# Attention and a silu feed-forward layer on one core: h of batches 2 to 7 by block products, and attention moved into the out layer's time

## The chip, the cores and the metric

The kernel runs on one core of a Trainium2 chip. Five engines work side by side, each through its own queue in order: PE (matrix products, with a weight-load queue PEld), DVE and ACT (element by element; ACT also has the sigmoid and silu tables), POOL (element by element, and it issues the loads) and SP (it issues transposes and stores). The metric is the device time of one execution in microseconds (us), here the median of several; smaller is better. A profiled execution also gives the span from the first to the last instruction.

## The reference

Eight batches of attention with 12 heads, 448 positions and 64 columns a head; the weights are a sigmoid, not a softmax. Then a feed-forward layer on 3584 rows:

```python
scores = scale * np.matmul(q, k.transpose(0, 1, 3, 2)) - np.log(S)   # S = 448
attn = 1.0 / (1.0 + np.exp(-scores))
x = np.matmul(attn, v).transpose(0, 2, 1, 3).reshape(B * S, H * D)   # 3584 x 768
h = x @ w_in                                                         # 768 x 2048
g = h * (1.0 / (1.0 + np.exp(-h)))
out = g @ w_out                                                      # 2048 x 768
```

## The kernel before

**Attention.** A quad is four heads of one batch; there are 24, numbered through the batches, three to a batch. Its q, k and v are loaded by POOL (`load`, line 71), as f16. The first quads' q and k are transposed on PE (`pe_transpose`), from quad 6 on by DMA: `dma_transpose` (line 158) copies rows together on ACT or DVE and SP issues the transpose. A unit is one of seven chunks of a quad's 448 keys: `scores(g, ch)` (line 169) makes four 64x64 matmuls into a score buffer `psc` (two buffers) and ACT takes the sigmoid into `attnT` (12 buffers). `values(g)` (line 193) multiplies seven chunks with v into two banks `pav`, and DVE copies them scaled into `xT` (line 218), the transposed x of a batch: six chunks of 128 columns by 448 positions. Buffers `pav`, `ph` and `po` share four PSUM banks (pool `ps_1`).

**h.** `h_unit(b, fc)` (line 229) makes one of 16 column groups of h of a batch: six matmuls over the chunks of x into `ph`; ACT takes the sigmoid, DVE multiplies it with `ph` into `gTr` (line 248), which holds g of two neighbouring batches.

**The out layer.** `out_set` (line 288) makes two row blocks of 128 rows of out at once by seven block products of eight matmuls each instead of eight (a Strassen scheme in Winograd's form): the operands are the quarters of `w_out` and of two blocks of g, with sums of them in `T1` to `T4` (`w_sums`, made once by DVE) and in `S1` to `S4` (made by DVE for each set). ACT copies the first product as `m1`; DVE adds the others up (`plus`, line 313) in `osb`, and SP stores `osb`. A pair of batches has seven row blocks, so three sets and one block left over; the left-over of an even pair is kept in `kept` and taken with that of the next pair: 14 sets.

**The order.** PE's order is written out by hand. `all_moe` (line 379) is one stream of the matmuls of h and the out layer, for a pair m of batches: h(2m), for m > 0 then the first set, h(2m+1), the other sets. `stretch(ns)` (line 398) takes as many matmuls of that stream as make ns (189 a matmul of h, 163 of out). The main loop at line 541 takes two units of scores, then perhaps one quad's values, perhaps one row copy (`rows_if_any`), then a stretch as long as `paces` says; before quad 6 (n = 42) it takes a stretch of 21500. After that, attention runs two batches ahead of h and lies in stretches of 2 to 3.4 us through h and out alike. POOL's order of loads follows from `after_transpose` and `after_values` (lines 431 and 440); POOL has eight loads under way at most.

Of the kernel before, what the change touches and what calls it, by code (L numbers as in the profile page):

```python
# [17 lines left out]
def kernel(  # L18
# [104 lines left out]
    def new_qkT(g):  # L123
        for name in ("k", "q"):
            qkT[name, g] = p4.tile([P, NCH, P], F16, tag=f"{name}T", name=f"{name}T")
# [32 lines left out]
    def dma_transpose(g, name, copy):  # L158
        if ("k", g) not in qkT:
            new_qkT(g)  # L160
        rows = p3.tile([P, NCH, 2, D], F16, tag=f"{name}r", name=f"{name}r")
# [31 lines left out]
    def values(g, end=NCH):  # L193
# [23 lines left out]
        for half in range(2):  # L217
            nc.vector.tensor_scalar_mul(xT[b][:, half * NQ + iq, :], pav[half][:, :S], SX)  # L218
# [10 lines left out]
    def h_unit(b, fc):  # L229
# [16 lines left out]
        tsig = p3.tile([P, S], F16, tag="tsig", name="tsig")  # L246
# [4 lines left out]
        yield 189  # L251

# [35 lines left out]
    def out_set(a1, rows1, a2, rows2, last=False):  # L288
        nonlocal hold
        lo, hi = slice(0, NHC), slice(NHC, NFC)  # L290
        osb = [p4.tile([P, DMODEL], F32, tag="osb", name="osb") for _ in range(2)]
        c11, c12 = (osb[0][:, nh * NO2 : (nh + 1) * NO2] for nh in range(2))
        c21, c22 = (osb[1][:, nh * NO2 : (nh + 1) * NO2] for nh in range(2))
        m1 = p2.tile([P, NO2], F32, tag="m1", name="m1")
        sg = [cpool.tile([P, NHC, P], F16, tag=f"S{i}", name=f"S{i}") for i in range(1, 5)]
# [7 lines left out]
        def product(a, w):  # L303
            po = ps_1.tile([P, 512], F32, tag="ps1", name="po")
            for fc in range(NHC):
# [3 lines left out]
                if fc < NHC - 1:  # L309
                    yield 163  # L310
            return po[:, :NO2]

        def plus(o, po, x, sign=ISX):
            nc.vector.scalar_tensor_tensor(  # L314
                out=o, in0=po, scalar=sign, in1=x, op0=ALU.mult, op1=ALU.add
            )

        nc.vector.tensor_sub(sg[2], a1[:, lo], a2[:, lo])
        nc.vector.tensor_add(sg[0], a2[:, lo], a2[:, hi])
        po = yield from product(a1[:, lo], wq[0][0])  # L320
        nc.scalar.activation(m1, po, AF.Copy, scale=ISX)  # L321
        nc.vector.tensor_sub(sg[1], sg[0], a1[:, lo])
        hold = False
        yield 163
        po = yield from product(a1[:, hi], wq[1][0])
# [5 lines left out]
        po = yield from product(sg[2], tw[3])  # L331
        plus(c22, po, m1)
        yield 163
# [5 lines left out]
        plus(c21, po, c22, -ISX)  # L339
# [15 lines left out]
    by_h1 = {3: 6, 6: 7, 9: 8}  # L355
    early = [h_unit(0, fc) for fc in range(2)]
    sums = w_sums()

    def moe_h(b):
# [71 lines left out]
    def after_transpose(g):  # L431
# [5 lines left out]
        elif g == 4:  # L437
            load("kq", 8)
# [153 lines left out]
```

## Time and profile before

| what | value |
|---|---|
| median of 3 runs | 381.67 us (380.77 to 382.28) |
| the profiled execution | 381.95 us |
| its span | 380.2 us, clock granted 1.00 |
| matmuls | 3083: 768 of h, 784 of out, 672 of scores, 672 of values, 168 transposes, 19 warm-ups |
| bytes moved by DMA | 42.80 MB, mean 113 GB/s |

How to read the profile's lines: a group is "line engine operation out<-in, shapes, xcount | busy us, mean ns of one | idle us of the engine just before them, and who ended it". The chain of work that ended last is "start us, us, engine, tile, line, xcount", in order of time. A wait is "engine, tile <- who was waited for: us in all, times, longest". The timeline is "start, us, engine, line, operation, tiles, shapes, xcount [idle before <- who ended it]". The durations of neighbours on one engine can overlap, as the next one enters while the last one drains.

### The profile page before, as it was taken

What the parts mean: (1) busy time and instruction counts of PE and PEld (TensorE: products, weight loads), DVE (VectorE), ACT (ScalarE), POOL (GpSimd) and SP (SyncE); (2) the same over time, 40 slices, a digit from 0 to 9 for tenths busy, and PEclk for the clock granted to TensorE, in tenths of its full rate; (3) what the DMA queues carried; (4) which work ended last, traced back from release to release, by engine and by line L of the source; (5) the groups of instructions that cost most, each with busy time, mean ns of one, the idle gap of its engine ahead of it and who ended that gap; (6) DMA issues with size and microseconds to landing.
All of it is one profiled execution on the core that took longest, in us unless ns stands there. A gap on an engine that the chain in (4) does not pass through costs nothing.

```text
span 380.2 us, 7666 instructions
## 1 busy us (share of the span) xinstructions
PE 370.8 (98%) x3083; PEld 186.0 (49%) x3083; DVE 235.2 (62%) x416; ACT 225.9 (59%) x329; POOL 93.5 (25%) x158
## 2 busy tenths in 40 slices
PE   7989999999999999999999999999999999999995
PEld 2444445545554445445555444544455444555563
DVE  2636646987565666566766647735757446656773
ACT  4988875757667764777434576477764776054000
POOL 8946325403752323122221303101100000000000
PEclk9999999999999999999999999999999999999999
DMA  7999999995999947945939949536347300110233
GB/s 125 177 185 204 205 204 171 133 140 110 165 241 216 151 56 99 173 54 69 162 67 183 132 78 121 71 86 74 48 85 97 84 3 2 50 34 0 82 85 83
DMA packets 66403, 42.80 MB, mean 113 GB/s; under 512 B 37056, under 2 KB 62912, under 8 KB 66368
## 3 DMA queue, kind: packets, MB, share of 16 engines
q0 software_dynamic: 28032, 22.59, 43.2%
q1 hardware_dynamic: 38112, 19.41, 28.5%
q8 instruction: 24, 0.39, 0.4%
q10 hardware_dynamic: 224, 0.33, 0.3%
q14 instruction: 11, 0.09, 0.1%
HBM read 45.61 MB, written 11.01 MB: 149 GB/s over the span
## 4 chain that ended last, share of the span: by engine, by line
PE 78%; DMA 13%; POOL 3%; DVE 3%; ACT 2%; issue 1%; ACTq 0%; POOLq 0%
PE po L306 34%; PE ph L235 29%; PE psc L176 8%; PE pav L207 6%; DMA w_in_sb<-in_moe_w_in_dram 5%; DMA w_out_sb<-in_moe_w_out_dram 5%; DMA qf<-in_q_dram 1%; DMA vf<-in_v_dram 1%; POOL kf L78 1%; DVE gTr L248 1%; DVE T L277 1%; POOL qf L78 1%; ACT qr L137 1%; POOL vf L78 1%; ACT attnT L183 0%
## 5 line engine op out<-in xcount | busy, mean ns | idle before, releaser
L183 ACT ACTIVATE attnT<-psc 128x896 f16<-128x896 f32 x168 | 144.2, 918 | 59.9 <-PE psc L176 59.8
L235 PE MATMUL ph<-xT,w_in_sb 128*128 128x448 f16 x768 | 153.2, 353 | 1.2 <-DMA w_in_sb<-in_moe_w_in_dram 1.2
L248 DVE TENSOR_TENSOR gTr<-ph,tsig 128x448 f16<-128x448 f32 x128 | 78.9, 623 | 70.1 <-ACT tsig L247 68.6
L235 PEld LDWEIGHTS <-w_in_sb 128*128 128x128 f16 x768 | 71.9, 98 | 77.1 <-issue 12.8
L247 ACT ACTIVATE tsig<-ph 128x448 f16<-128x448 f32 x128 | 68.6, 547 | 54.4 <-PE ph L235 53.7
L78 POOL DMA_DIRECT2D vf<-in_v_dram x48 | 28.9, 624 | 136.4 <-PE pav L207 136.4
L306 PEld LDWEIGHTS <-S 128*128 128x128 f16 x448 | 42.3, 98 | 33.9 <-issue 6.8
L314 DVE SCALAR_TENSOR_TENSOR osb<-po,osb 128x384 f32<-128x384 f32 x70 | 37.6, 554 | 25.2 <-PE po L306 24.5
L176 PE MATMUL psc<-qT,kT 64*64 64x448 f16 x672 | 50.7, 362 | 0.9 <-ACT attnT L183 0.3
L218 DVE TENSOR_SCALAR xT<-pav 128x448 f16<-128x448 f32 x48 | 27.7, 619 | 31.4 <-PE pav L207 31.4
L306 PE MATMUL po<-T,S 128*128 128x384 f16 x224 | 40.6, 327 | 0.1
L306 PEld LDWEIGHTS <-gTr 128*128 128x128 f16 x304 | 28.7, 98 | 23.4 <-issue 5.0
L306 PE MATMUL po<-w_out_sb,S 128*128 128x384 f16 x224 | 39.9, 326 | 0.0
L207 PE MATMUL pav<-attnT,vf 64*64 64x448 f16 x672 | 37.5, 349 | 0.2 <-DVE gTr L248 0.2
L78 POOL DMA_DIRECT2D qf<-in_q_dram x46 | 27.7, 613 | 39.4 <-DVE qr L162 16.7
L306 PE MATMUL po<-w_out_sb,gTr 128*128 128x384 f16 x192 | 34.7, 327 | 0.0
L78 POOL DMA_DIRECT2D kf<-in_k_dram x50 | 30.3, 618 | 7.8 <-DVE kr L162 4.3
L176 PEld LDWEIGHTS <-kT 64*64 64x64 f16 x672 | 14.2, 104 | 31.0 <-issue 29.0
L207 PEld LDWEIGHTS <-vf 64*64 64x64 f16 x672 | 20.1, 107 | 12.3 <-issue 1.5
L314 DVE SCALAR_TENSOR_TENSOR osb<-po,m 128x384 f32<-128x384 f32 x42 | 23.1, 551 | 3.9 <-PE po L306 2.5
L306 PE MATMUL po<-T,gTr 128*128 128x384 f16 x112 | 21.4, 326 | 0.0
L321 ACT ACTIVATE m<-po 128x384 f32<-128x384 f32 x14 | 6.9, 492 | 24.0 <-PE po L306 24.0
(41 smaller groups left out, 130.8 us busy)
## 6 DMA issues: line engine op xcount, KB each, us to landing
out_dram<-osb SPq DMA_DIRECT2D x54, 192.0 KB, 3.0
vf<-in_v_dram POOLq DMA_DIRECT2D x48, 112.0 KB, 4.4
kf<-in_k_dram POOLq DMA_DIRECT2D x46, 112.0 KB, 5.4
qf<-in_q_dram POOLq DMA_DIRECT2D x46, 112.0 KB, 5.8
w_in_sb<-in_moe_w_in_dram POOLq DMA_DIRECT2D x4, 768.0 KB, 10.6
w_out_sb<-in_moe_w_out_dram POOLq DMA_DIRECT2D x4, 768.0 KB, 17.1
kT<-kr SPq DMA_TRANSPOSE x18, 5.8
qT<-qr SPq DMA_TRANSPOSE x18, 5.6
```

The source lines that it names most:

```text
L78: nc.gpsimd.dma_start(flat[name, g][half * HP : (half + 1) * HP, :, c0:c1].rearrange("p i c d -> p i (c d)"), source[name][b, h0 : h0 + 2] ...
L137: nc.scalar.activation(o, i, AF.Copy)
L176: nc.tensor.matmul(psc[own, j, :S], qkT["k", g][rows, ch, own], qkT["q", g][rows, :, own], start=True, stop=True,)
L183: nc.scalar.activation(attnT[g, ch], psc[:, :, :S], AF.Sigmoid, bias=NEG_LOG_S, scale=QKSCALE)
L207: nc.tensor.matmul(pav[half][j * D : (j + 1) * D, :S], flat["v", g][own, j, ch, :], at[own, j, :], start=(ch == 0), stop=(ch == NCH - 1),)
L218: nc.vector.tensor_scalar_mul(xT[b][:, half * NQ + iq, :], pav[half][:, :S], SX)
L235: nc.tensor.matmul(ph[:, :S], w_in_sb[:, cc, fc * P : (fc + 1) * P], xT[b][:, cc, :], start=(at == 0), stop=(at == NCC - 1),)
L247: nc.scalar.activation(tsig, ph[:, :S], AF.Sigmoid, bias=0.0, scale=ISX)
L248: nc.vector.tensor_mul(gTr[:, fc, (b % 2) * S : (b % 2) * S + S], ph[:, :S], tsig)
L306: nc.tensor.matmul(po[:, :NO2], a[:, fc, :], w[:, fc, :], start=(fc == 0), stop=(fc == NHC - 1))
L314: nc.vector.scalar_tensor_tensor(out=o, in0=po, scalar=sign, in1=x, op0=ALU.mult, op1=ALU.add)
L321: nc.scalar.activation(m1, po, AF.Copy, scale=ISX)
```

## The change

- h of the pairs m = 1, 2, 3 is made by `h_pair` for both batches at once, with seven block products over quarters of `w_in` and of x of the two batches. Each of its eight rounds makes a column group of 128 of the upper and of the lower half: seven products of three matmuls, where two batches by two column groups by six chunks were 24. g of a round comes from four silus on ACT and five f32 adds on DVE, and a copy of the first product on ACT. Part of a round (`late`) is taken in the next round, and that of the last round in the first product of the first out set (`between`). h of batches 0 and 1 is made as before.
- Sums of `w_in` (`w_in_sums`): six operations on POOL, between loads, three on DVE in h of batch 0, three on DVE in place after h of batch 1. Sums of x (`x_sums`): four on DVE for each chunk pair of a pair of batches, in buffers of `attnT`.
- No attention is taken inside `h_pair`. The units of the next pair's batches lie in the out sets of the pair before, and values in two pieces of four and three rounds. Before quad 6 there is a stretch of 12500 instead of 21500.
- ACT's table changes to silu ahead of each `h_pair` and back to sigmoid behind it: seven table loads instead of one.
- The out set behind `h_pair` gets its first sums made inside the loop, and takes its second and third products in the other order. `kept` is made on DVE instead of ACT; one of twelve xT copies of a later pair is on ACT.
- Loads: the four pieces of `w_out` in another order, two of them and q and k of quads 6 and 7 each behind one of POOL's sums; q and k of quad 9 after the transposes of quad 5, from quad 10 on when the rows of the quad two before are copied. Row copies of quads 6 to 8 begin in h of batch 0 instead of h of batch 1; later ones start within the quad three before instead of after its values.
- Buffers: transposed q and k three instead of four, rows two instead of three, `osb` three instead of four; `m1`, `tsig` and the new copies share three.

The diff, cut to its core:

```diff
         for half in range(2):
-            nc.vector.tensor_scalar_mul(xT[b][:, half * NQ + iq, :], pav[half][:, :S], SX)
+            if b > 2 and b % 2 == 1 and iq == NQ - 1 and half == 0:
+                nc.scalar.activation(
+                    xT[b][:, half * NQ + iq, :], pav[half][:, :S], AF.Copy, scale=SX
+                )
+            else:
+                nc.vector.tensor_scalar_mul(xT[b][:, half * NQ + iq, :], pav[half][:, :S], SX)
+        if b > 2 and b % 2 == 1:
+            x_sums(b // 2, iq)
...
+    def x_sums(m, iq):
+        b11, b21 = (xT[2 * m][:, half * NQ + iq, :] for half in range(2))
+        b12, b22 = (xT[2 * m + 1][:, half * NQ + iq, :] for half in range(2))
+        t = [p12.tile([P, 2, S], F16, tag="attnT", name="xs") for _ in range(2)]
+        t1, t2, t3, t4 = (t[i // 2][:, i % 2, :] for i in range(4))
+        for o, x, y in ((t1, b12, b11), (t2, b22, t1), (t4, b21, t2), (t3, b22, b12)):
+            nc.vector.tensor_sub(o, x, y)
+        xs[m, iq] = t1, t2, t3, t4
...
+        sw[3] = a21
+        for c in range(HCC):
+            eng = nc.vector if c == HCC - 1 else nc.gpsimd
+            eng.tensor_add(sw[1][:, c], a21[:, c], a22[:, c])
+            yield
+            eng.tensor_sub(sw[2][:, c], sw[1][:, c], a11[:, c])
+            yield
+            eng.tensor_sub(sw[4][:, c], a12[:, c], sw[2][:, c])
+            yield
+        for c in range(HCC):
+            nc.vector.tensor_sub(sw[3][:, c], a11[:, c], a21[:, c])
...
+        sides = {
+            1: (w_in_sb[:, lo, top], lambda c: x[0][:, c, :]),
+            2: (w_in_sb[:, hi, top], lambda c: x[0][:, HCC + c, :]),
+            3: (sw[4], lambda c: x[1][:, HCC + c, :]),
+            4: (w_in_sb[:, hi, low], lambda c: xs[m, c][3]),
+            5: (sw[1], lambda c: xs[m, c][0]),
+            6: (sw[2], lambda c: xs[m, c][1]),
+            7: (sw[3], lambda c: xs[m, c][2]),
+        }
+        def product(n, ps, i, first):
+            a, bs = sides[n]
+            for c in range(HCC):
+                nc.tensor.matmul(
+                    ps,
+                    a[:, c, i * P : (i + 1) * P],
+                    bs(c),
+                    start=(first and c == 0),
+                    stop=(c == HCC - 1),
+                    skip_group_check=True,
+                )
+                yield 189
+        def silu(side, odd, i, src):
+            nc.scalar.activation(
+                gTr[:, side * NHC + i, odd * S : (odd + 1) * S], src, AF.Silu, scale=ISX
+            )
+        def late(i, y, z, p1, u2, u3):
+            silu(1, 1, i, u3)
+            if m < B // 2 - 1 and i < 4:
+                rows_of_quad(
+                    2 * NQ * (m + 1) + 1 + i // 2,
+                    "kq"[i % 2],
+                    (act_copy, nc.vector.tensor_copy)[i % 2],
+                )
+            yield from product(3, z, i, False)
+            nc.vector.tensor_add(u2, z, u2)
+            silu(0, 1, i, u2)
+            yield from product(4, y, i, False)
+            nc.vector.tensor_add(p1, y, p1)
+            silu(1, 0, i, p1)
+        sg = []
+        begun = {}
+        def begin(i):
+            xb = ps_1.tile([P, 512], F32, tag="ps1", name="hx")[:, :S]
+            yield from product(1, xb, i, True)
+            p1 = p3.tile([P, S], F32, tag="m1", name="p1")
+            nc.scalar.activation(p1, xb, AF.Copy)
+            begun[i] = xb, p1
+        EARLY = NHC - 2
+        behind = None
+        yield from begin(0)
+        for i in range(NHC):
+            end = i == NHC - 1
+            if not end:
+                yield from begin(i + 1)
+            xb, p1 = begun[i]
+            y = ps_sc.tile([P, 2, 512], F32, tag="pssc", name="hy")[:, 0, :S]
+            yield from product(6, y, i, True)
+            u2 = p3.tile([P, DMODEL], F32, tag="osb", name="u2")[:, :S]
+            nc.vector.tensor_add(u2, y, p1)
+            if end:
+                nc.vector.tensor_add(behind[5], behind[2], behind[5])
+                set_sums(sg, 2, 0, EARLY)
+            z = ps_1.tile([P, 512], F32, tag="ps1", name="hz")[:, :S]
+            yield from product(5, z, i, True)
+            if behind is not None and not end:
+                yield from late(*behind)
+            yield from product(2, xb, i, False)
+            silu(0, 0, i, xb)
+            yield from product(7, y, i, False)
+            u3 = cpool.tile([P, S], F32, tag="S2" if end else "S4", name="u3")
+            nc.vector.tensor_add(u3, y, p1)
+            if i == EARLY:
+                for s in (1, 3):
+                    sg.append(cpool.tile([P, NHC, P], F16, tag=f"S{s}", name=f"S{s}"))
+            else:
+                nc.vector.tensor_add(u3, z, u3)
+            if end:
+                yield from late(*behind)
+                set_sums(sg, 2, EARLY)
+                set_sums(sg, 0, 0, EARLY)
+            behind = i, y, z, p1, u2, u3
+        sg.insert(1, cpool.tile([P, NHC, P], F16, tag="S2", name="S2"))
...
+        def rest():
+            yield from late(*behind)
+            nc.scalar.activation(warm, warm, AF.Sigmoid)
+            set_sums(sg, 0, EARLY)
+            set_sums(sg, 1)
+            h_done.update((2 * m, 2 * m + 1))
...
+        if tail:
+            po = yield from product(sg[2], tw[3])
+            plus(c22, po, m1)
...
+    rows_at = {14: (6, "k"), 16: (6, "q"), 18: (7, "k"), 21: (7, "q"), 24: (8, "k"), 28: (8, "q")}
...
+            if b == 0 and fc >= NFC - 3:
+                next(in_sums)
             if b == 1:
-                if fc >= 2:
-                    next(sums)
-                if fc in by_h1:
-                    for name in ("k", "q"):
-                        dma_transpose(by_h1[fc], name, act_copy)
-
-    def moe_set(m, g):
-        step = out_set(block(g), row_blocks(m, g), block(g + 1), row_blocks(m, g + 1))
+                next(sums)
+                if fc == 9:
+                    first_sg.extend(
+                        cpool.tile([P, NHC, P], F16, tag=f"S{i}", name=f"S{i}") for i in (1, 2, 3)
+                    )
+                if fc in (9, 11, 13):
+                    set_sums(first_sg, {9: 2, 11: 0, 13: 1}[fc])
+            if b * NFC + fc in rows_at:
+                rows_of_quad(*rows_at[b * NFC + fc], act_copy)
...
+                nc.vector.tensor_scalar_mul(kept[:, fcs], block(NCH - 1)[:, fcs], scale)
+            if m == 0 and g == 2 and i in (36, 44, 52):
+                next(in_sums)
...
+            tail = []
             if m == 0:
-                yield from moe_set(m, 0)
+                yield from moe_h(0)
+                yield from moe_h(1)
+                tail = [None, *first_sg]
+            else:
+                yield from h_pair(m, tail)
+            yield from moe_set(m, 0, tail)
...
+            load_w_out(1, 0)
+            load_w_out(1, 1)
         elif g == 2:
             load("v", 5)
-            load_w_out(1, 0)
-            load_w_out(1, 1)
-            load("kq", 6)
-            load("kq", 7)
+            for what in ("k", 6), ("q", 6), (0, 1), ("k", 7), ("q", 7), (0, 0):
+                next(in_sums)
+                (load_w_out if what[0] == 0 else load)(*what)
...
+    def rows_of_quad(g, name, copy):
+        dma_transpose(g, name, copy)
+        if name == "q" and 7 < g < NQB - 2:
+            load("kq", g + 2)
...
+    PACE, BURST, ROUND, SPARE = 1600, 590, 200, 2400
+    sets = 7 * NHC * 163
+    h_at = [(2 * NFC * NCC - 8) * 189 + 3 * sets]
+    for m in (1, 2):
+        h_at.append(h_at[-1] + 7 * NHC * HCC * 189 + (3 + m % 2) * sets)
+    AHEAD = 4
+    ends = [2 * NT_B, 4 * NT_B + AHEAD, 6 * NT_B + AHEAD, 8 * NT_B]
+    values_left = 2 * NT_B
+    stretch(PACE)
     for n in range(NT_B + 3, len(units), 2):
         burst = units[n : n + 2]
         if n == 2 * NT_B:
             values_if_any()
-            stretch(21500)
+            stretch(12500)
         for u in burst:
             scores(*u)
-        values_if_any()
+        had = values_if_any()
         rows_if_any()
         for g, ch in burst:
+            if ch == NCH - 3 and g >= 6 and g % 6 < 4 and g + 3 < NQB:
+                later.extend(((g + 3, "k"), (g + 3, "q")))
             if ch == NCH - 1:
-                waiting.append(g)
+                waiting.extend(((g, 0, NCH),) if n < 2 * NT_B else ((g, 0, 4), (g, 4, NCH)))
         if n in (24, 30):
             transposes(4 + (n - 24) // 6, "k")
         elif n in (26, 32):
             transposes(4 + (n - 26) // 6, "q")
-        stretch(paces[1] if 1 not in ready else paces[n // NT_B])
-    for g in waiting:
-        values(g)
+        if n < ends[0]:
+            stretch(PACE)
+            continue
+        m = bisect.bisect(ends, n)
+        if n + 2 == ends[m]:
+            nc.scalar.activation(warm, warm, AF.Silu)
+        dense = h_at[m - 1] - SPARE - done
+        due = done
+        stretch((dense + values_left * ROUND) / ((ends[m] - n) // 2) - had * ROUND)
+        values_left -= had
+        if n + 2 == ends[m]:
+            while waiting:
+                values_if_any()
+                stretch(SPARE / 3)
+            values_left = 2 * NT_B
+            while 2 * m not in h_done:
+                done += next(stream)
+            due = done
+            stretch(3000)
```

More of the change, by code (lines that the diff above doesn't have):

```diff
@@ L245, in h_unit @@
             h_done.add(b)
[L246 removed]
+        tsig = p3.tile([P, 2 * S], F16, tag="m1", name="tsig")[:, :S]
         nc.scalar.activation(tsig, ph[:, :S], AF.Sigmoid, bias=0.0, scale=ISX)
@@ L330, in out_set @@
         yield 163
-        po = yield from product(sg[2], tw[3])
-        plus(c22, po, m1)
-        yield 163
+        if not tail:
+            po = yield from product(sg[2], tw[3])
+            plus(c22, po, m1)
+            yield 163
         po = yield from product(sg[1], tw[2])
@@ L391, in all_moe @@
                 yield from out_set(
-                    kept, row_blocks(m - 1, g), block(g), row_blocks(m, g), m == B // 2 - 1
+                    kept,
+                    row_blocks(m - 1, g),
+                    block(g),
+                    row_blocks(m, g),
+                    1.0,
+                    last=(m == B // 2 - 1),
                 )
```

108 lines of the change are left out of this document (64 added, 44 removed).

## The prediction, on record before the result

> **What bounds the kernel now.** I read the page's shares and slices first, then the chain of work that ended last in order of time, then the waits.
>
> ```profile
> span 380.2 us, 7666 instructions
> PE 370.8 (98%) x3083; PEld 186.0 (49%) x3083; DVE 235.2 (62%) x416; ACT 225.9 (59%) x329; POOL 93.5 (25%) x158
> PEclk9999999999999999999999999999999999999999
> PE 78%; DMA 13%; POOL 3%; DVE 3%; ACT 2%; issue 1%; ACTq 0%; POOLq 0%
> ```
>
> PE is busy 98% at the full granted clock; DVE and ACT have some 40% to spare. A busy PE may still be waiting, so the chain has to tell.
>
> ```profile
> 57.30 5.39 DMA qf<-in_q_dram
> 79.29 0.50 PE psc L176 x8
> 115.61 2.56 PE ph L235 x13
> 118.17 0.50 PE psc L176 x8
> 121.93 1.32 PE pav L207 x28
> 330.33 18.16 PE ph L235 x96
> 348.49 27.31 PE po L306 x168
> 375.83 0.56 DVE osb L314
> ```
>
> Loads are in the chain until 63 us; from 79 us to 375.8 it is almost wholly matmuls. 96 h matmuls in 18.16 us are 0.189 us each, 168 out matmuls in 27.31 us are 0.163 us each. That is streaming without holes: with 6 matmuls a unit the 96 contain 16 starts into a fresh bank, and 96 x 0.189 = 18.14 leaves nothing for them. Two attention units of scores take 0.50, seven rounds of values 1.32, and each turn to scores and back about 0.1 (13 x 0.189 = 2.46 of 2.56). The waits agree:
>
> ```profile
> PE psc L176 <- ACT attnT L183: 0.3, 1, 0.3
> ```
>
> That is PE's only wait for a score buffer in the run. So removed matmuls shorten the run one for one, until another engine or a load is late.
>
> **What the change does to that sum.**
>
> *Removed.* Batches 2 to 7 had 6 x 16 x 6 = 576 h matmuls. Three pairs by seven products, eight column groups and three chunks have 3 x 168 = 504. 72 x 0.189 = **-13.6**. Out matmuls, scores, values and warm-ups keep their counts. The order of instructions has two more turns to scores: +0.2.
>
> *The block loop.* One of its eight rounds a pair has 21 matmuls, 21 x 0.189 = 3.97 us, with no attention between. Beside them stand five 448-column adds on DVE, four silus and one copy on ACT.
>
> ```profile
> L248 DVE TENSOR_TENSOR gTr<-ph,tsig 128x448 f16<-128x448 f32 x128 | 78.9, 623 | 70.1 <-ACT tsig L247 68.6
> L314 DVE SCALAR_TENSOR_TENSOR osb<-po,osb 128x384 f32<-128x384 f32 x70 | 37.6, 554 | 25.2 <-PE po L306 24.5
> L247 ACT ACTIVATE tsig<-ph 128x448 f16<-128x448 f32 x128 | 68.6, 547 | 54.4 <-PE ph L235 53.7
> 57.49 1.15 DVE L218 TENSOR_SCALAR xT<-pav 128x448 f16<-128x448 f32 x2 [0.24 <-PE pav L207]
> 330.17 4.13 PE L235 MATMUL ph<-xT,w_in_sb 128*128 128x448 f16 x21
> 331.51 0.54 ACT L247 ACTIVATE tsig<-ph 128x448 f16<-128x448 f32 x1 [8.99 <-PE ph L235]
> ```
>
> No row has an f32 add of 448 columns. Below it is gTr (623 ns, f16 out), above it the osb row scaled to 448, 554 x 448/384 = 646; I take 0.62, as gTr has the width. Two in a row take 1.15, so the second adds 0.53. DVE needs 2.7 to 3.1 of 3.97, ACT 5 x 0.547 = 2.7 at most. The tightest link: after the seventh product, u3 = y + p1, then z is added, and only then may the third product write z again, which PE reaches nine matmuls (1.70) later. The first tsig starts at 331.51, 0.21 after six matmuls from 330.17 have passed, so the link is 0.21 + 0.62 + 0.62 = 1.45. Margin 0.25. A row copy on DVE (0.61) stands behind the next add and misses this link; k's copy goes to ACT, behind a silu. I take 0 here; bounds 0 and, if an add takes 0.80, 0.1 x 24 = 2.4.
>
> *Into and out of the loop.* The last sums of x need the last values. For batches 2-3 and 4-5, 19 or 20 out matmuls (3.1 us) lie between; for batches 6-7 one, and six h matmuls, and the third chunk is wanted 1.7 us after the values. The chain is 0.21 + 0.62 and two dependent sums. Their 448 f16 columns cost about 0.38, an estimate from the rows below (681 at 1024, 548 at 768, so 0.52 ns a column): 1.6 in all, plus up to two osb operations queued ahead (1.1). Taken 0.5, and 0.4 for the first rounds; bounds 0 and 2.
>
> ```profile
> L318 DVE TENSOR_TENSOR S<-gTr 128x1024 f16<-128x1024 f16 x12 | 8.2, 681 | 0.0
> L277 DVE TENSOR_TENSOR T<-w_out_sb 128x768 f16<-128x768 f16 x8 | 4.4, 548 | 0.0
> L422 ACT ACT_TABLE_LOAD x1 | 1.3, 1283 | 1.5 <-PEq L576 1.5
> L321 ACT ACTIVATE m<-po 128x384 f32<-128x384 f32 x14 | 6.9, 492 | 24.0 <-PE po L306 24.0
> L162 DVE COPY kr<-kf 128x896 f16<-128x896 f16 x15 | 9.1, 608 | 0.0
> ```
>
> Six more table loads are 7.7 us of ACT. The one ahead of each loop has 4 us or more between the last sigmoid's burst and the loop's first copy. The one behind each loop delays m1 by 1.3; the bank of that product is asked for again four products (5.2 us) later, so it is hidden.
>
> *DVE as a whole:* 40 adds for 32 gTr and 12 sums of x a pair, (8 x 0.62 + 12 x 0.38) x 3 = 29, six w_in sums 4, kept 3, less four row copies and three xT, 4: 267 us of 370. Still not the bound.
>
> *Attention inside the out layer.* Of the 63 bursts of two units that come after the first two batches', 60 now fall between out matmuls; by the order the tightest (last pair) have 8 to 11 out matmuls between, 9 x 0.163 + 0.50 + 0.2 = 2.2 us.
>
> ```profile
> 141.90 3.34 ACT L183 ACTIVATE attnT<-psc 128x896 f16<-128x896 f32 x4
> 143.67 0.38 PE L176 MATMUL psc<-qT,kT 64*64 64x448 f16 x4 [0.30 <-ACT attnT L183]
> ```
>
> Four sigmoids in 3.34 are 0.84 each, 1.7 a burst; with m1 (0.49) 2.2. So it fits, without room in the bursts that hold an m1. The second row prices a miss: bursts 1.6 us apart behind an m1 cost 0.30. Ten m1 lie in these stages: bounds 0 and 3; taken 0.5, as only the last pair's bursts are that tight.
>
> *Start-up.* The order of PE is unchanged until after values of quad 5; then scores of quad 6 come 33 h and 17 out matmuls sooner: 79.29 - 6.2 - 2.8 = 70.3.
>
> ```profile
> 43.42 0.88 POOL L114 DMA_DIRECT2D w_out_sb<-in_moe_w_out_dram  x1 [2.91 <-DMA w_in_sb<-in_moe_w_in_dram]
> 53.08 1.18 POOL L78 DMA_DIRECT2D kf<-in_k_dram  x2 [0.19 <-issue]
> 57.30 0.59 POOL L78 DMA_DIRECT2D qf<-in_q_dram  x1 [3.04 <-DMA w_out_sb<-in_moe_w_out_dram]
> 61.15 0.59 POOL L78 DMA_DIRECT2D qf<-in_q_dram  x1 [3.27 <-DMA w_out_sb<-in_moe_w_out_dram]
> 59.30 0.54 ACT L247 ACTIVATE tsig<-ph 128x448 f16<-128x448 f32 x1 [0.59 <-PE ph L235]
> 65.39 0.62 DVE L248 TENSOR_TENSOR gTr<-ph,tsig 128x448 f16<-128x448 f32 x1 [1.02 <-ACT tsig L247]
> 68.23 0.97 ACT L247 ACTIVATE tsig<-ph 128x448 f16<-128x448 f32 x2
> 76.91 4.81 SPq L163 DMA_TRANSPOSE kT<-kr  x1
> qT<-qr SPq DMA_TRANSPOSE x18, 5.6
> masks.py:199 POOL TENSOR_SCALAR_AFFINE_SELECT ident<-ident 128x128 f16<-128x128 f16 x1 | 0.3, 288 | 0.1
> ```
>
> Six w_in sums of 1024 columns now stand in POOL's queue between the loads of k, q and the last two w_out pieces. They can start when w_in has landed (43.4). One takes between 0.68 (DVE's price, row above) and 8 x 0.288 = 2.3 (POOL's own row of 128 columns); I take 2.3, being POOL's. With eight half loads (0.59) and two w_out issues (0.9) the last piece leaves at 43.4 + 13.8 + 6.5 = 63.7; pieces landed 3.85 apart (57.30 to 61.15), so with about 1 us of latency it lands at 68.6, where it had landed by 61.15. The Trainium skill, GPSIMD Engine Reference, section 3.1, speaks against such sums: a two-input add of 2048 f32 columns is given as 4497 ns there against 2293 on DVE. By it one sum would be an estimated 2.25 us; no run here shows it yet. By that figure the term below stays; by DVE's price the piece leaves at 54, the term is 0 and the whole sum -12.0.
>
> Behind that load: (1) DVE's fifth w_out sum, behind the gTr of h unit 20 (65.39), idle from 66.0 to 68.6. PE has four banks, fills units 21 to 24 until about 68.9, and unit 25 waits until the gTr of 21 frees its bank at 69.7: 0.8. DVE then needs 1.0 of each 1.13, so it does not slip further. (2) ACT's copy of k of quad 8, behind unit 24 (about 69.2), whose load follows the w_out piece: 1 to 2 late, and ACT's sigmoids with it. (3) q of quad 6: copied behind unit 16 (59.30), transposed from 60.8, landing at 66.4 by the median, at 71.2 if the issue is held 4.8 as at 76.91; wanted at 70.3. The three fall into the same microseconds. Taken 2.0; bounds 0 (at 0.68 a sum; no gain, as PE's waits name none of these loads now) and 7 (transposes and loads delaying each other by one such hold).
>
> **Sum:** -13.6 + 0.2 + 0.9 + 0.5 + 2.0 = **-10.0**. The profiled execution took 381.95 (1.75 around its span of 380.2), 0.3 above the median of 381.67; from the median 371.7. With no stall at all 368.3.
>
> **The rivals.**
>
> *Late start-up (376.5).* The sums on POOL hold loads so long that k of 8, q of 6 and w_out are all late, 7 instead of 2. For: SP's transpose at 76.91 was already held 4.8. Against: the same bytes of w_out had landed by 61.15.
>
> *Attention too dense (375.5).* ACT is late in most of the 63 bursts, 0.07 each more than taken: +4. For: m1 leaves no room in the tight bursts. Against: 1.7 of 2.2.
>
> *Each product pays for its start (381.5, no change).* The loops have 3 x 56 products of three matmuls, each behind a wait for a bank; at 0.06 a start they eat 10 us, and the change gives nothing. Against: the 16 starts in 18.16 us cost nothing.
>
> *The block loop is DVE's (slower, 388).* If the five adds with the waits between them take 0.93 each, a round takes 4.65 instead of 3.97, PE loses 0.68 in each of 24 rounds, 16.3, and 371.7 becomes 388. It decides from 0.42 a round, the forecast's 10.0 over 24: a round above 4.39 is slower than before. For: one u3, two score banks, and adds that depend on each other. Against: 0.62 measured for such an operation, and neighbours on DVE overlap.
>
> **How the numbers follow.** A measurement can tell about 0.5% (1.9 us) from no change. Forecast 0.62 (own range 368 to 375), late start-up 0.15, dense attention 0.08, paid starts 0.04, loop on DVE 0.11. Faster 0.85, same 0.04, slower 0.11. The range reaches over the first three cases: 367.8 (all stalls nought, 0.5 for the scatter) to 378.5 (start-up at 7 and the other bounds in part).
>
> **What would show it.** h matmuls 696 in all, and a chain of PE from some 75 us to the end. In the block loops 21 matmuls in 4.0 us and hardly a wait of PE for DVE's u or p; if PE waits there for DVE over 0.3 a round, the loop's margin is wrong. W sums on POOL near 2.3 us each, DVE's w_out sum waiting for a DMA near 66, scores of quad 6 at 70 to 73. PE's wait for attnT under 1 us in all. The sum is wrong if the span lost is not 13.4 less PE's waits, read from the waits.

## The result, and the profile after

The changed kernel takes 378.8 us (median of 6 runs, 378.05 to 386.54) against 381.6: a ratio of 0.9924, 95% interval 0.9906 to 0.9943. So it is faster, by 2.8 (0.8%) where 10.0 was forecast. (Executions more than 1.5% above the fastest of the same kernel are left out of every ratio here, which leaves 3 of 10 of e5 and 5 of 10 of e7, and nothing is read from the profiles of e5, e6 and e9, which are of such executions.) The profiled execution took 379.05, its span is 377.2. The head of its page:

```profile
span 377.2 us, 7672 instructions
...
PE 361.0 (96%) x3011; PEld 180.6 (48%) x3011; DVE 264.5 (70%) x489; ACT 249.6 (66%) x364; POOL 105.9 (28%) x164
...
PEclk9999998999999999999999999999999999999999
```

The 72 matmuls are gone (3083 before), and DVE's total is near the 267 of the forecast. But slice 7, at 57 to 66 us, has a lower clock, and PE's waits have new names. The view of the waits, PE's own and one of DVE's (total, times, longest):

```profile
PE ph L243 <- DVE xT L224: 2.6, 2, 2.4
PE hy L320 <- DVE u L372: 2.5, 2, 1.3
...
PE ph L243 <- DVE gTr L256: 1.3, 1, 1.3
...
PE hz L320 <- ACT gTr L331: 0.5, 2, 0.2
...
DVE u L372 <- DMA out_dram<-osb: 6.3, 4, 2.7
```

**At the start-up** DVE releases PE late, twice. DVE's and POOL's timelines, then the busy times at 58 to 67 us (PE, PEld, DVE, ACT, POOL, granted clock, DMA share, GB/s), of after and of before:

```profile
55.79 3.66 DVE L284 TENSOR_TENSOR W<-w_in_sb 128x1024 f16<-128x1024 f16 x1
59.37 0.61 DVE L256 TENSOR_TENSOR gTr<-ph,tsig 128x448 f16<-128x448 f32 x1
59.91 2.83 DVE L286 TENSOR_TENSOR W<-W,w_in_sb 128x1024 f16<-128x1024 f16 x1
62.66 1.14 DVE L224 TENSOR_SCALAR xT<-pav 128x448 f16<-128x448 f32 x2
...
64.26 0.68 DVE L288 TENSOR_TENSOR W<-w_in_sb,W 128x1024 f16<-128x1024 f16 x1
```

```profile
56.75 2.14 POOL L286 TENSOR_TENSOR W<-W,w_in_sb 128x1024 f16<-128x1024 f16 x1
58.82 1.21 POOL L79 DMA_DIRECT2D qf<-in_q_dram  x2
60.05 2.13 POOL L288 TENSOR_TENSOR W<-w_in_sb,W 128x1024 f16<-128x1024 f16 x1
...
64.20 1.22 POOL L79 DMA_DIRECT2D qf<-in_q_dram  x2
```

```profile
58.00:67.00 9.00, 5.12 (x22) 2.03 (x19) 7.94 (x9) 2.44 (x5) 8.99 (x12) 0.84 1.26 150
```

```profile
58.00:67.00 9.00, 9.00 (x49) 4.66 (x48) 6.30 (x13) 6.15 (x11) 5.55 (x10) 1.00 1.14 167
```

Such a sum on DVE takes 0.68 when POOL only issues loads (64.26) and 3.66 and 2.83 beside POOL's sums; each long one ends 0.56 us after a sum of POOL's. The gTr and the xT behind them free PE's banks: PE idles 3.9 of 9.0 us, and a clock of 0.84 takes 1.4 more, 1.7 with the 0.5 us of half clock behind 67. That is 5.6 where the forecast had 2.0.

**In the first rounds of the loops** the second u2 (L372) waits for a store. DVE, the issue of the stores, PE:

```profile
139.68 0.62 DVE L372 TENSOR_TENSOR u<-hy,p 128x448 f32<-128x448 f32 x1 [2.71 <-DMA out_dram<-osb]
```

```profile
133.24 3.43 SPq L455 DMA_DIRECT2D out_dram<-osb  x4
```

```profile
140.35 0.73 PE L320 MATMUL hy<-xs,w_in_sb 128*128 128x448 f16 x3 [1.30 <-DVE u L372]
```

u2 is a tile of tag osb, which shares three buffers with the out rows; the ones it gets are still being stored by the set ahead of the loop. PE names 2.5 + 0.5 us of waits in the loops. Read instead as the distance from one matmul's start to the next less the usual 0.189, the stops with their restarts are 4.2 in the loops and 6.0 in the start-up, 10.2 together; -13.4 for the matmuls and +10.2 give -3.2, and the span fell by 3.0.

### The profile page after: what moved, and what is told of

Same layout as the page of the kernel before. It is cut to its first block, busy times and chain, and to the rows that moved or that the text cites. A ratio compares the mean times of both kernels' runs of the same rounds, so it can differ in the third digit from the quotient of the medians.

```text
span 377.2 us, 7672 instructions
## 1 busy us (share of the span) xinstructions
PE 361.0 (96%) x3011; PEld 180.6 (48%) x3011; DVE 264.5 (70%) x489; ACT 249.6 (66%) x364; POOL 105.9 (28%) x164
## 4 chain that ended last, share of the span: by engine, by line
PE 73%; DMA 13%; POOL 5%; DVE 5%; issue 2%; ACT 2%; DVEq 0%; ACTq 0%; SPq 0%; POOLq 0%
PE po L462 33%; PE hy L320 9%; PE psc L177 8%; DMA w_in_sb<-in_moe_w_in_dram 6%; PE hz L320 6%; PE pav L208 6%; PE hx L320 5%; PE ph L243 5%; DMA out_dram<-osb 3%; DMA w_out_sb<-in_moe_w_out_dram 2%; POOL kf L79 2%; DMA vf<-in_v_dram 2%; DVE xs L272 1%; DVE osb L472 1%; POOL qf L79 1%
## 5 line engine op out<-in xcount | busy, mean ns | idle before, releaser
L243 PE MATMUL ph<-xT,w_in_sb 128*128 128x448 f16 x192 | 41.3, 364 | 5.0 <-DVE xT L224 2.6
L331 ACT ACTIVATE gTr<-u 128x448 f16<-128x448 f32 x48 | 27.6, 575 | 27.7 <-DVE u L344 24.4
L320 PEld LDWEIGHTS <-w_in_sb 128*128 128x128 f16 x288 | 28.1, 98 | 29.3 <-issue 3.4
L462 PE MATMUL po<-w_out_sb,S 128*128 128x384 f16 x224 | 41.5, 327 | 0.0
L208 PE MATMUL pav<-attnT,vf 64*64 64x448 f16 x672 | 41.1, 350 | 0.3 <-DVE gTr L256 0.2
L320 PE MATMUL hy<-xs,w_in_sb 128*128 128x448 f16 x144 | 35.1, 352 | 2.6 <-DVE u L372 2.5
L462 PE MATMUL po<-w_out_sb,gTr 128*128 128x384 f16 x192 | 36.6, 327 | 0.0
L320 PE MATMUL hx<-xT,w_in_sb 128*128 128x448 f16 x144 | 34.6, 352 | 0.0
L320 PEld LDWEIGHTS <-W 128*128 128x128 f16 x216 | 21.1, 98 | 20.5 <-issue 1.2
L243 PEld LDWEIGHTS <-w_in_sb 128*128 128x128 f16 x192 | 18.0, 100 | 25.8 <-issue 10.5
L256 DVE TENSOR_TENSOR gTr<-ph,tsig 128x448 f16<-128x448 f32 x32 | 19.5, 621 | 13.0 <-ACT tsig L255 12.9
```

The lines of the kernel that those rows point to most:

```text
L208: nc.tensor.matmul(pav[half][j * D : (j + 1) * D, :S], flat["v", g][own, j, ch, :], at[own, j, :], start=(ch == 0), stop=(ch == NCH - 1),)
L243: nc.tensor.matmul(ph[:, :S], w_in_sb[:, cc, fc * P : (fc + 1) * P], xT[b][:, cc, :], start=(at == 0), stop=(at == NCC - 1),)
L256: nc.vector.tensor_mul(gTr[:, fc, (b % 2) * S : (b % 2) * S + S], ph[:, :S], tsig)
L320: nc.tensor.matmul(ps, a[:, c, i * P : (i + 1) * P], bs(c), start=(first and c == 0), stop=(c == HCC - 1), skip_group_check=True,)
L331: nc.scalar.activation(gTr[:, side * NHC + i, odd * S : (odd + 1) * S], src, AF.Silu, scale=ISX)
L462: nc.tensor.matmul(po[:, :NO2], a[:, fc, :], w[:, fc, :], start=(fc == 0), stop=(fc == NHC - 1))
```

## The experiments

Two theories of where the gain went. **A:** DVE's sums are held by POOL's, because both read two tiles of SBUF, and u2 by the stores; both are stalls of their own. **B:** they are symptoms of late transfers (w_out, k, q), so that taking them away only shows the next wait. Ratios are to the kernel before on the same chip.

| kernel | median us (lowest to highest, runs) | ratio, 95% interval |
|---|---|---|
| e1_sums_apart | 375.84 (374.72 to 384.72, 5) | 0.983, 0.979 to 0.988 |
| e2_u2_own | 374.64 (373.11 to 377.55, 4) | 0.981, 0.976 to 0.987 |
| e3_both | 374.42 (372.43 to 378.79, 4) | 0.978, 0.973 to 0.983 |
| e5_dve_sums | 380.52 (372.55 to 385.17, 10) | 0.984, 0.979 to 0.989 |
| e6_swap | 376.46 (372.73 to 382.01, 6) | 0.983, 0.978 to 0.989 |
| e7_swap_dve | 383.13 (377.52 to 385.33, 10) | 0.996, 0.991 to 1.000 |
| e8_swap_only | 375.04 (371.32 to 382.41, 6) | 0.979, 0.972 to 0.985 |
| e9_no_v | 374.22 (370.40 to 376.07, 6) | 0.978, 0.975 to 0.982 |
| e10_sums_no_v | 374.90 (371.68 to 380.84, 6) | 0.980, 0.977 to 0.984 |
| e11_hold | 374.44 (370.39 to 377.23, 6) | 0.977, 0.972 to 0.982 |
| e12_sums_hold | 375.60 (371.79 to 382.54, 6) | 0.981, 0.977 to 0.985 |
| e4_before_pool | 410.44 (one run) | |
| e13_before_dve | 381.38 (380.53 to 382.60, 12) | 1.000, 0.999 to 1.001 |
| e14_before_pool6 | 394.03 (393.19 to 395.43, 5) | 1.034, 1.031 to 1.036 |
| e15_before_both | 394.04 (391.92 to 394.86, 5) | 1.031, 1.029 to 1.034 |
| e16_before_late | 382.00 (381.64 to 383.85, 11) | 1.002, 1.000 to 1.003 |

### The two stalls, one at a time

**e2_u2_own:** u2 from a pool in which nothing is being stored.

```diff
-            u2 = p3.tile([P, DMODEL], F32, tag="osb", name="u2")[:, :S]
+            u2 = p12.tile([P, S], F32, tag="attnT", name="u2")
```

> The changed kernel with u2 of the block loop in free buffers of attnT instead of those of osb, which wait until they are stored. Store theory: DVE's four waits for the store (6.3 us) go, and with them PE's holes of 1.4 and 0.4 us in the first rounds of the first two loops: 375.2 +- 0.8. Rival, DVE is behind there anyway (four osb operations and the sums of x stand ahead): the holes stay above 1 us a loop, 377.5 to 379.

In its profile (of the fastest of the four, 373.11) no wait of PE in the loops is left, and one round's seven products follow the last in 3.97 us:

```profile
135.01 0.73 PE L320 MATMUL hz<-xT,W 128*128 128x448 f16 x3
...
138.98 0.73 PE L320 MATMUL hz<-xT,W 128*128 128x448 f16 x3
```

By the distances between starts, the loops' stops fall from 4.2 to 0.4 us. From 0.992 to 0.981 is 4.2 us of 381.6, which the intervals leave open by some 2 us. That the stores cause the loops' stops is settled.

**e1_sums_apart:** DVE's three sums into the first out set of pair 0, away from POOL's.

```diff
-            if b == 0 and fc >= NFC - 3:
-                next(in_sums)
-            if m == 0 and g == 2 and i in (36, 44, 52):
+            if m == 0 and (g == 0 and i in (12, 20, 28) or g == 2 and i in (36, 44, 52)):
```

> The changed kernel with DVE's three sums of w_in moved from the end of h of batch 0 into the first out set of the first pair, 20 us after POOL's last sum. Port theory: DVE's sums, with both operands in SBUF, could not run beside POOL's (3.66 and 2.83 us instead of 0.68); apart, each takes 0.68, PE's waits for gTr and xT near 60 us (1.3 and 2.4) and the half-speed matmuls behind them (about 2) go, 373.2 +- 0.8. Late-loads theory (POOL's queue delays w_out, k and q, as the prediction had it): the holes near 60 us stay or move to w_out's sums near 67 us, 377 to 379.

The sums take 0.68 and the hole (a stretch in which PE is idle) at 58 to 63 is gone, but another of PE opens at 68, of 3.8 (waits of e1, PE; the loops' wait stays too):

```profile
PE ph L243 <- DVE gTr L256: 3.8, 1, 3.8
PE hy L320 <- DVE u L372: 2.6, 2, 1.3
```

The median lies between the two expectations. By the ratios e1 is clearly faster than the changed kernel (0.979 to 0.988 against 0.991 to 0.994), by some 3.5 us: taken apart alone, the sums do pay. The profile is of the slowest execution in the ratio, 379.93, and in it the new hole takes back what the old one cost.

**e3_both:** both edits.

> Both edits. If the two causes are separate and are all that went wrong, the gains add: 369.8 +- 1.2, which is 13.4 below the kernel before plus under 2 of stalls. If the second only hides behind the first (less DVE delay early, but the same end), 372 to 374.

DVE's timeline and PE's of e3 name the new wait, the forecast's own w_out piece, which left POOL at 61.0 behind its sums:

```profile
69.28 0.56 DVE L431 TENSOR_TENSOR w_out_sb<-w_out_sb 128x768 f16<-128x768 f16 x1 [4.21 <-DMA w_out_sb<-in_moe_w_out_dram]
```

```profile
70.43 3.05 PE L243 MATMUL ph<-xT,w_in_sb 128*128 128x448 f16 x9 [2.98 <-DVE gTr L256]
```

In after this wait lies inside the stall of the sums. The two repairs do not add: alone they bring some 3.5 and 4.2 us, together 5.5, and 0.978 is no clear gain on e2's 0.981. Nor is every meeting gone: DVE's first sum of w_out in e3 (at 59.52) takes 2.02 in place of 0.55 beside POOL's last sum, here without a wait of PE.

### Is the late w_out the last cause?

**e5_dve_sums:** both edits, and all nine sums on DVE between out matmuls, none on POOL, so that the loads go out at once. **e6_swap:** e3 with the needed piece of w_out loaded three sums sooner. **e8_swap_only:** e2 with that swap. **e7_swap_dve:** e5 with it.

```diff
-            for what in ("k", 6), ("q", 6), (0, 1), ("k", 7), ("q", 7), (0, 0):
+            for what in ("k", 6), ("q", 6), (0, 0), ("k", 7), ("q", 7), (0, 1):
```

> Both edits, and POOL's six sums too on DVE, in the first two out sets of the first pair: POOL's queue holds loads alone. Port theory: DVE has room there (0.6 a sum), nothing waits for the loads, so the time is that of both edits, +- 0.8. Late-loads theory: loads come up to 13 us sooner, and what is left of holes between 55 and 85 us goes: 1 to 3 us below both edits.

> The kernel of e3_both (DVE's three sums of w_in away from POOL's, the loop's sum in an attnT buffer) with one thing more: of the two late pieces of w_out, the one that DVE's fifth sum reads ((0, 0): left columns, upper half) is loaded where the other one was, three sums of POOL earlier. Nothing else of the order of loads changes. Theory A (the last cause is that piece, which left POOL at 61.0 and landed at 69.2 in e3_both): the sum at 69.28 no longer waits 4.2 us, PE's hole of 3.15 us and the window of half clock behind it (1.6 us in matmuls) go, so the time is 374.4 - 4.7 = 369.7, bounds 368.5 to 371. Rival B (the transfer is late because the DMA engines are shared, and the loads of k and q or the transposes that the swap does not touch are next): PE waits for qT or kT by 2 us or more in the first 90 us, time 372 to 375. Rival C (the second late piece now holds the twelfth sum at 74): a wait of DVE for DMA w_out above 1 us at 74 to 77, time 371 to 373.

> The kernel of e2_u2_own with the swap of the two late pieces of w_out of e6_swap, but with DVE's three sums of w_in still beside POOL's. Theory A (the two start-up stalls, DVE behind POOL at 56 to 63 and the late w_out at 66 to 69, lie behind one another and are paid once): the sums still take 3.7 and 2.8 us, PE's hole of 2.5 us before 65 and its half clock stay, time 374.6, within 1 of e2_u2_own; so neither repair alone gives anything, and both give 5. Rival B (the late piece also cost something in e2_u2_own): 372.5 or less. Rival C (DVE's long sums are not from POOL but from the loads around them, which the swap moves by little): the same time as A here, but then e6_swap does not gain either.

> The kernel of e5_dve_sums (all nine sums of w_in on DVE, none on POOL) with the swap of the late pieces of w_out. If w_out's late piece was what cost e5_dve_sums its gain: DVE's wait for DMA w_out of 3.5 us goes and the time is 369 to 371. If the loads of q and the transposes behind them are what came late there (PE waited 7.9 us for qT in 5 waits): those waits stay, and the time stays at 374 to 380, spread widely from run to run.

For e5 neither expected time was met: the median of all ten is 380.5, and its ratio of 0.984 is no better than e3's 0.978. Theory A of e6 is wrong: 0.983, not 369.7 us. Of e8 the price is as expected (375.0), but with e6 no better, it shows nothing of a second repair. In e7 the wait for w_out is gone, and others stand there; its waits:

```profile
PE psc L177 <- DMA qT<-qr: 4.5, 3, 2.2
PE pav L208 <- DVE osb L472: 2.1, 1, 2.1
...
DVE osb L472 <- DMA out_dram<-osb: 4.7, 1, 4.7
```

So even with POOL free of sums the transposed q and the stores come late, and the kernel is hardly faster than before. By the ratios the swap cost e7 some 4.5 us against e5, on three and five executions from two chips; whether that is so, and why, stays open.

**e9_no_v** and **e10_sums_no_v:** e6 and e8 without the loads of v from quad 8 on, whose values then come from an older v.

```diff
+            if name == "v" and g > 7:
+                flat[name, g] = flat[name, g - 3]
+                continue
```

> The kernel of e6_swap with the loads of v left out from quad 8 on (the values of those quads are worked out from the v of an earlier quad, in the same instructions), so that from some 72 us on a quarter of the loads is missing. In the e6_swap and e7_swap_dve runs PE waited 2 us and more for qT<-qr at 70 to 124 us, and SP took 4 to 6 us to issue a transfer that took it 1.2 before. Theory A (with the start-up repaired, the loads and the transposing transfers of k and q set the pace until 125 us): without those loads PE's waits for qT go below 0.5 us in total, SP's issues go back to 1.2 to 2 us, and the time is that of the nominal stream, 366 to 369, with a spread of under 2 us. Rival B (the transposing transfers are late by their own chain, row copies of ACT and DVE that wait their turn): the waits stay and the time stays at 374 to 377.

> The kernel of e8_swap_only (DVE's three sums of w_in beside POOL's, as in the changed kernel) with the same loads of v left out. By theory A the transfers no longer set the pace here either, so the difference to e9_no_v is the price of the sums' meeting alone: PE's holes of 2.9 us before 65 and a window of half clock worth 1.9, 371 to 373.5, that is 4 to 5.5 above e9_no_v. By rival B, or if the hole is given back by a transfer that is then in time, the two are within 1.5 us of each other.

Theory A failed in both: they stay at 374 to 375, as the rival had it, and e10 still waits for q, so the loads of v alone are not what delays it:

```profile
PE psc L180 <- DMA qT<-qr: 3.9, 2, 2.4
```

**e11_hold** and **e12_sums_hold:** e6 and e8 with more h ahead of batch 2's scores.

```diff
-            stretch(12500)
+            stretch(17500)
```

> The kernel of e6_swap (both repairs and the swap; nothing left out) with PE given 17.5 us of h before the first scores of batch 2 in place of 12.5 (one number). The loads and transposes of quads 6 to 8 keep their places, which go by h's units, so the scores of quad 6 to 8 ask for them some 5 us later; the later bursts stand 0.5 us closer together. Theory A (what is left over, once the sums are apart, is that PE asks for k and q before they have landed: e6_swap and e9_no_v lost 2 to 6 us in holes at 70 to 120 and a window of half clock): the holes of 70 to 90 go, those of 100 to 120 shrink, the time is 368 to 371. Rival B (the loads follow the bursts, so that later scores only move the same waits): holes of 3 us and more stay at 75 to 125, 374 to 377, as in e6_swap.

> The kernel of e8_swap_only (DVE's three sums beside POOL's as in the changed kernel, the loop's sum in an attnT buffer, the swap) with the same 17.5 us. By theory A the difference to e11_hold is the price of the sums' meeting alone, 2.9 us of holes before 65 and 1.9 of half clock, so 371 to 374, 3 to 5 above e11_hold. By rival B, or if the hole only hides the transfers, within 1.5 us of e11_hold.

Rival B again: e11 waits for q between 110 and 120 us instead (first fence), e12 for the sums as after does (second), and their intervals overlap.

```profile
PE psc L177 <- DMA qT<-qr: 3.4, 1, 3.4
```

```profile
PE ph L243 <- DVE xT L224: 2.4, 1, 2.4
...
PE ph L243 <- DVE gTr L256: 1.1, 1, 1.1
```

### The sums alone, in the kernel before

The kernel before agrees with itself within about 2 us on the chip of e13 to e16 and has no hole at 60 us, so there one stall does not hide behind another.

**e4_before_pool:** an addition on POOL in every burst from quad 6 on.

```diff
+        if n >= 2 * NT_B:
+            nc.gpsimd.tensor_add(scratch, w_in_sb[:, 0, :1024], w_in_sb[:, 1, :1024])
```

> The kernel before with one addition more on POOL in each burst from quad 6 on: two f16 tiles of 1024 columns in SBUF, added into a tile that nobody reads (nothing is left out). It asks which of DVE's instructions an addition on POOL lengthens. Theory A (the two engines share a way into SBUF that DVE needs for two operands from SBUF and POOL holds for its whole addition): POOL's additions take 2.1 to 2.2 us; those of DVE's that read two SBUF operands (S<-gTr at 0.68, T<-w_out_sb at 0.55, and osb<-po,osb if the second operand counts) take up to 2.1 us more where they meet one, while gTr<-ph,tsig (one operand in PSUM, 0.62) and xT<-pav (0.62) stay within 3 per cent; time 382 to 386. Rival B (POOL and DVE only share bandwidth): every kind of DVE instruction beside an addition is some tens of per cent longer, POOL's additions too. Rival C (they do not meet; the long sums of the changed kernel come from DMA writes into w_in or w_out): nothing of DVE's changes, and the time is 381.6.

The costliest groups of e4 (mean ns behind the busy time):

```profile
L248 DVE TENSOR_TENSOR gTr<-ph,tsig 128x448 f16<-128x448 f32 x128 | 78.9, 623 | 70.2 <-ACT tsig L247 68.7
L315 DVE SCALAR_TENSOR_TENSOR osb<-po,osb 128x384 f32<-128x384 f32 x70 | 37.6, 554 | 21.6 <-PE po L307 20.5
...
L320 DVE TENSOR_TENSOR S<-gTr 128x1024 f16<-128x1024 f16 x14 | 19.2, 1371 | 0.0
...
L277 DVE TENSOR_TENSOR T<-w_out_sb 128x768 f16<-128x768 f16 x8 | 10.4, 1300 | 0.0
L162 DVE COPY kr<-kf 128x896 f16<-128x896 f16 x15 | 9.1, 610 | 0.0
```

Theory A, and clearly: what reads two tiles of SBUF becomes about twice as long or more in the mean of the groups shown (S from 683, T from 548), what reads one, or one beside PSUM, stays as before (623, 554, and 610 against 608). Only the time was far off, 410 (one execution) where 382 to 386 was expected; that the 63 additions also hold up POOL's loads was not taken apart. The Trainium skill states this in SBUF — State Buffer, section "SBUF: two separate sides": DVE with two SBUF inputs and a GpSimd instruction that reads SBUF need the same pair of ports, whoever starts first holds it for its whole instruction, and the other stands still. The traces agree on which instructions are held. By it a sum of DVE's that starts beside one of POOL's is up to an estimated 2.13 us longer, the length of POOL's; the first sum in after was 2.98 longer and had begun before POOL's, so the measurement differs on who goes first.

**e13 to e16:** the parts of the changed start-up, into scratch tiles of before: DVE's three sums (e13), POOL's six behind the loads (e14), both (e15), POOL's six between the loads (e16).

```diff
+            if b == 0 and fc >= NFC - 3:      # e13, e15
+                next(dve_sums)
...
+            for _ in pool_sums:               # e14, e15: behind load("kq", 7)
+                pass
...
+            for what in (1, 0), (1, 1), ("k", 6), ("q", 6), ("k", 7), ("q", 7):   # e16
+                next(pool_sums)
+                (load_w_out if what[0] == 1 else load)(*what)
```

> The kernel before with three sums of w_in more on DVE (128x1024 f16, into a tile that nobody reads), behind the last three columns of batch 0's h, where the changed kernel has them; POOL has none. Nothing is left out. Theory A (alone they take 0.68 each and DVE has room): each takes 0.67 to 0.70 and the time is 381.5 to 382.3. Rival B (the place itself is too tight for DVE, whatever POOL does): PE waits for gTr or xT there by 1 us or more, 383 to 385.

> The kernel before with six sums of w_in on POOL (2.13 each), back to back behind the loads of k and q of quads 6 and 7, so that no load of the first 70 us leaves later; DVE has none. Theory A (POOL's sums disturb only such instructions of DVE as read two tiles of SBUF, and DVE has few there; T<-w_out_sb perhaps): 381.5 to 383. Rival B (POOL's sums cost by themselves): 384 or more, with DVE's gTr, xT or ACT's instructions longer in the stretch of 45 to 62 us.

> The kernel before with DVE's three sums of e13_before_dve and POOL's six of e14_before_pool6, in the same stretch. Theory A (DVE is held behind POOL's sums): DVE's sums that meet one take 2 to 3.7 us in place of 0.68, PE stands 2 to 3 us at gTr or xT and a window of half clock follows, so 385 to 388. Rival B (what costs is DVE's or POOL's work by itself): the excesses of e13 and e14 add up, under 383.5.

> The kernel before with POOL's six sums between its loads of that stretch (one ahead of each piece of w_out and of k and q of quads 6 and 7, as the changed kernel has them), and none on DVE: the last of these loads leave POOL near 60 us in place of 47. Theory A (late loads cost in the stretch of 60 to 85 what the trace of e9 showed: ACT, whose row copies stand in its order, waits for k or q of quad 7, and PE for ACT): 1 to 5 us, 383 to 387. Rival B (the loads have enough slack in the kernel before, whose scores of quad 6 come after 21.5 us of h in place of 12.5): 381.5 to 382.5.

e13: 0.68 each and no time. e16: POOL's six sums meet none of DVE's, and cost 0.2%. It did not make a load late, as its expectation had it: its last q left POOL at 59.96, and before's at 61.15, since POOL waits there for other transfers; so late loads were not tried by it. e14 and e15 do not tell apart what they were meant to: POOL reached its sums only at 60 us, behind loads that wait for their buffers, and met DVE's sums of w_out instead. They cost 12.5 us all the same. DVE, POOL and PE of e14, and ACT:

```profile
66.97 1.94 DVE L277 TENSOR_TENSOR T<-w_out_sb 128x768 f16<-128x768 f16 x1
69.36 1.94 DVE L277 TENSOR_TENSOR T<-w_out_sb 128x768 f16<-128x768 f16 x1
```

```profile
66.17 2.32 POOL L367 TENSOR_TENSOR W<-w_in_sb,W 128x1024 f16<-128x1024 f16 x1
68.57 2.31 POOL L363 TENSOR_TENSOR W<-w_in_sb 128x1024 f16<-128x1024 f16 x1
```

```profile
PE ph L235 <- DVE gTr L248: 9.7, 6, 4.7
```

```profile
79.11 0.95 ACT L137 ACTIVATE kr<-kf 128x896 f16<-128x896 f16 x1 [6.64 <-DMA kf<-in_k_dram]
```

DVE's 0.55 becomes 1.94 in step with POOL, and PE loses 5.0 of its 9.7 us in five waits at these sums. The sixth, 4.7, is the forecast's item (2): k of quad 8, loaded behind POOL's sums, holds ACT's copy and with it the sigmoids. So a meeting costs PE about 1.0 us there, where DVE stands between PE and its banks, and a load that is late behind POOL's sums can cost more than any of them.

## Why the prediction was wrong, step by step

- **Removed and added matmuls, -13.4:** right (3083 to 3011), and so is the steady loop, 21 matmuls in 3.97 with adds of 0.61 to 0.62. The rivals "paid starts" and "loop on DVE" are out.
- **Attention inside the out layer, +0.5:** about 0; no wait of PE for attnT is among its waits.
- **Into the loop and first rounds, +0.9:** failed. The step counted u2 as an add of 0.62 whose inputs are early and did not ask whose buffer it takes: an osb, with four stores under way. The stops are 4.2 us; e2 takes 3.8 of them away.
- **Start-up, +2.0:** failed. It put DVE's three sums there at nothing; they stand only in DVE's total, as "six w_in sums 4" us, 0.68 each. That price came from rows of a kernel in which POOL had no such sums. Beside POOL's sums two of DVE's took 6.5 in place of 1.4; 5.6 us by the waits and the clock, 6.0 by the starts. The first scores of quad 6 came at 76.60, 6.3 behind the 70.3 of a start-up without a stall. e4 and e14 show the mechanism, e13 and e16 that neither engine's sums cost more than 0.2% by themselves.
- **POOL's sums at 2.3, the last piece of w_out landing at 68.6:** 2.13 to 2.16, and 69.4 in after. The landing is near because two errors partly cancel: issued by 63.0 and 6.4 us from there, in place of 63.7 and 4.9. DVE's wait for it is hidden in after, and in e3 it is 4.2 of DVE and 3.0 of PE, where the forecast had 2.6 and 0.8.
- **The range and the rivals:** 378.8 lies 0.3 beyond the upper end of the range. The rival "late start-up" had the place and nearly the size, 7 where 6.0 was lost, but by late loads and not by DVE; for the loops' first rounds the bound was 2, and 4.2 came on top.
- With both stalls repaired e3 has a ratio of 0.978, 0.973 to 0.983; the forecast was 371.7 of 381.67, 0.974. So the sum without the two missed terms was not far off, though e3's start-up still loses 4.2 by the starts, for the late w_out, where 2.0 was forecast.

**Open:** the start-up's price within the changed kernel. Taken away alone (e1) it brings some 3.5 us; taken away behind u2's repair (e3 against e2, e6 against e8, e11 against e12) it brings nothing that the intervals show, and a late transfer stands in its place: w_out in e3, q at 70 to 124 in e7, e10 and e11. The stall itself differs from trace to trace: PE's holes are 1.3 and 2.4 us in after, one of 2.4 in e2, and in e10, where DVE's sums took 0.73, 2.08 and 1.77, one of 0.95. SP needs 1.2 to 2.9 us to issue a transposing transfer in after, up to 6.0 in e10, and up to 5.1 in the kernel before, where PE waits for no q after the start. What lengthens it was not found; the loads of v are not it alone.

## What to carry to other kernels

Before work is moved to POOL, look at what DVE runs beside it: with two operands in SBUF on both sides they take turns, and a row's price holds only for what POOL did beside it. For every new tile ask which buffers its tag shares and what still reads them; a store counts as a reader until it has landed. And where a stage has several late suppliers, repair them in a kernel without the others, or each repair will only show the next wait.

## What the runs showed of the hardware

- DVE's sum at 55.79 began 0.96 us ahead of POOL's, while POOL issued loads, and was held until that sum had ended (58.89) all the same. An issue of loads by itself did not hold it: the third sum (64.26) took 0.68 beside one.
- PE's clock halves for windows of 3.41 us (6.83 in e12) after some holes: one followed the holes of 1.3 and 2.4 us in after and the one of 3.0 in e3, none the single holes of 1.3 us in the loops, and none one of 3.4 in e11, so the length of the hole alone does not decide it. In after matmuls start 0.373 us apart in the window in place of 0.189, which is 1.7 us on top of the idle time. The Trainium skill, TensorE: Matmul & The Clock Gate, section "What's actually happening", gives a free-running window of 3413 ns and half clock after one of them idle; the length agrees, but here holes shorter than a window were enough.
